# Scores of both head groups in one piece of TensorE, the first batch by halves, and product 1 of the next block between products 5 and 3

## The chip, the core and the metric

The program runs on one core of a Trainium2 chip. The metric is the device time of one execution in microseconds (us), the median of several executions. A core has TensorE (PE, matmuls; its weight loads are listed apart as PEld), VectorE (DVE), ScalarE (ACT), GpSimd (POOL), and SyncE (SP), which here issues all DMAs. They run side by side and wait for each other by semaphores; each works through its own instructions in a fixed order.

## What is computed

Attention over 32 memory slots, then two feed-forward layers, all in float32:

```python
a = softmax(phi, axis=2)                          # (8 batches, 8 heads, 576 tokens, 32 slots)
k_m = einsum('bhsm,bhsd->bhmd', a, k); v_m = einsum('bhsm,bhsd->bhmd', a, v)
scores = matmul(q, k_m.transpose(0, 1, 3, 2)) / sqrt(64)
x = matmul(softmax(scores), v_m)                  # tokens: 8 batches x 576, heads joined to 512
r = maximum(x @ w_in, 0);  x = (s * r * r + b) @ w_out      # 512 -> 2048 -> 512
h = x @ w1;  out = (h * sigmoid(1.702 * h)) @ w2            # 512 -> 2048 -> 512
```

(`softmax` stands for the reference's maximum, exponential and division by the sum plus 1e-9; `w1` and `w2` are the second layer's `moe2_w_in` and `moe2_w_out`.)

## The kernel before

The work has four stages, each of eight blocks; a block is one batch of 576 tokens, always handled as two halves of 288 columns (`HS`). Matmuls of full size keep two parts of each operand, a high and a low one, and take three passes: high·high, high·low, low·high. The conversions `hi` and `lo` that make these parts run on ACT or DVE.

- **Stage 1, attention and the first matrix.** For a batch and each of two groups `g` of four heads, `slots` makes the slot softmax and a tile `km` (64 rows of it per group hold the keys). `attend` multiplies `km` with the queries: eight small matmuls of 64 x 32 weights and 288 columns (rows of `km` given by `g`, columns by the head `p`, one half `u` of the tokens each), into one PSUM tile `a`; these are *the scores of one head group*. DVE turns them (`st`), takes the maximum, subtracts, ACT takes the exponential, DVE sums, divides and turns back (`aT`), and `hi` and `lo` make `ah` and `al`. `matrix` folds the values into the first weight matrix: eight matmuls of 64 x 32 and 512 columns into a PSUM tile `vw`, from which ACT makes `mh` and DVE `ml`; four times a batch. `step` then does 12 full-size matmuls (`mh`·`ah`, `mh`·`al`, `ml`·`ah`) into a PSUM tile `h`; ACT (or DVE) applies the maximum with zero and SP stores the result. There are 16 steps a batch. While batch b is in its steps, the slots and scores of batch b+1 are made.
- **Stages 2 and 4, `down`.** 2048 to 512 by seven products instead of eight (two levels of additions replace one product). Each product has four quarters `q` of 12 full-size matmuls. Products 1, 6, 5 and 3 add up in one PSUM tile X, 2 in Z, 7 and 4 in Y. After 1, 6 and 5, X is copied out by ACT before the next product may add to it: `leave` does it, in stage 2 with two ACT instructions (tiles `a`, `u2`, `u4`; `u` in the rows), in stage 4 with one.
- **Stage 3, `up`.** 512 to 2048 with the same seven products, in four quarters; the change does not touch it.

PSUM holds four tiles (`"ps": 4`, two banks each) for all of this. The order of everything is written out by a planner (class `Order`): each operation has a due time and a set of tiles that it reads and writes, and the planner assigns engine and place by its own costs. Where an operation can run on ACT or DVE, it takes the one with the smaller "start + cost x `WEIGHT`". So a due time or a weight moves many instructions. Before the first batch's steps, PE is kept busy with dummy matmuls (`warm`), which the planner puts into gaps until the operation `last` is placed.

Of the kernel before, what the change touches and what calls it, by code (L numbers as in the profile page):

```python
# [18 lines left out]
P = 128  # L19
# [8 lines left out]
class Order:  # L28
# [9 lines left out]
    LAG = {"pe": 0.7, "sync": 2.5, "dve": 0.25, "act": 0.25, "pool": 0.25}  # L38
    WEIGHT = {"dve": 1.0, "pool": 1.6, "act": 1.0}

# [112 lines left out]
class Net:  # L153
# [249 lines left out]
    def slots(self, b, g, due, lead=8):  # L403
# [42 lines left out]
        def norm():  # L446
            s = self.t(rs, [P, 1])
            nc.vector.tensor_scalar(s, T[z][:, 0, 128:129], EPS, None, op0=ALU.add)
            nc.vector.reciprocal(s, s)
            nc.vector.tensor_scalar(self.t(a, [P, P]), T[z][:, 0, 0:128], s, None, op0=ALU.mult)  # L450

        self.on_dve(d + 5, 60, norm, (z,), (a, rs), count=4)

# [8 lines left out]

    def attend(self, b, g, due):
        nc, T = self.nc, self.T
        S, J = self.S, self.S // 32
        qs = [("t", ("q", b, p)) for p in range(4)]
        if g == 0:
            for p, k in enumerate(qs):
                self.dma(due - 8 + 0.5 * p, lambda k=k: self.t(k, [P, S]), lambda p=p: self.a["q"][b, p], (), (k,))
        d = due  # L470
        ps, sm, sm2 = ((x, ("a", b, g, x)) for x in ("ps", "sm", "sm"))
        sm2 = ("sm", ("a2", b, g))
        st, aT = ("t", ("st", b, g)), ("t", ("aT", b, g))
        km, o = ("km", (b, g)), slice(64 * g, 64 * g + 64)

        def score():
            out = self.pst(ps)
            for u in range(2):
                for p in range(4):
                    w = slice(32 * p, 32 * p + 32)  # L480
                    nc.tensor.matmul(out[w, u, 0:self.HS], T[km][o, w], T[qs[p]][o, u * self.HS:(u + 1) * self.HS], start=True, stop=True)

        def turn():
            x = self.t(st, [P, J, 32]).rearrange("p J m -> p (J m)")
            for u in range(2):
                c = slice(u * self.HS, (u + 1) * self.HS)
                nc.vector.transpose(x[:, c], T[ps][:, u, 0:self.HS])

        def with_slots(e, m, op):
            e.tensor_tensor(T[st], T[st], T[m].unsqueeze(2).to_broadcast([P, J, 32]), op=op)  # L490
# [7 lines left out]
        self.pe(d, 2200, score, (*qs, km), (ps,))  # L498
        self.on_dve(d + 1, self.HS, turn, (ps,), (st,), count=2)
        self.on_dve(d + 2, S, lambda: nc.vector.tensor_reduce(self.t(sm, [P, J]), T[st], axis=AX.X, op=ALU.max), (st,), (sm,))  # L500
        self.on_dve(d + 2, S, lambda: with_slots(nc.vector, sm, ALU.subtract), (sm,), (st,), port=True)
        self.on_act(d + 3, S, lambda: nc.scalar.activation(T[st], T[st], AF.Exp, scale=0.125), (), (st,))
        self.on_dve(d + 4, S + 200, total, (st,), (sm2,))
        self.on_dve(d + 4, S, lambda: with_slots(nc.vector, sm2, ALU.mult), (sm2,), (st,), port=True)
        self.on_dve(d + 5, S, lambda: nc.vector.transpose(self.t(aT, [P, S]), T[st].rearrange("p J m -> p (J m)")), (st,), (aT,))
        ah, al = ("t", ("ah", b, g)), ("t", ("al", b, g))
        self.hi(d + 6, S, lambda: self.t(ah, [P, S], F32R), lambda: T[aT], (aT,), (ah,))
        self.lo(d + 6.5, S, lambda: self.t(al, [P, S], F32R), lambda: T[aT], lambda: T[ah], (aT, ah), (al,))

# [21 lines left out]
    def step(self, b, pi, u, due):  # L531
# [12 lines left out]

        self.pe(due, 12 * HS, mm, (*m, *ats[0], *ats[1]), (h,))
        self.order.add(due + 0.5, [
# [22 lines left out]
    def down(self, name, src, s, due, prior, first):  # L569
# [5 lines left out]
        G = [[("t", (x, name, s, q)) for x in "ABCDE"] for q in range(4)]  # L575
        pos = {1: 0, 2: 1, 6: 2, 7: 3, 5: 4, 3: 5, 4: 6}
        to = {1: X, 2: Z, 6: X, 7: Y, 5: X, 3: X, 4: Y}
# [172 lines left out]
    def warm(self, begin):  # L750
# [18 lines left out]
        else:  # L769
            self.pe(-5, 0, last, (x, ("t", ("al", 0, 0))))  # L770

    def plan(self):
# [8 lines left out]
        for b in range(B):  # L781
            s0 = b * B1
            if b == 0:
                for g in range(2):
                    self.slots(0, g, -42 + 4 * g, 10)
                    self.attend(0, g, -28 + 4 * g)
                self.warm(False)
            for j in range(4):
# [117 lines left out]
```

## Time and profile before

| | |
|---|---|
| median of 3 executions | 1437.73 us (1436.1 to 1439.28) |
| the profiled execution's own time | 1438.46 us |
| its span, first to last instruction | 1436.4 us |
| mean granted TensorE clock | 0.992 of full |
| stage 1 on PE | to 341.6 us |
| stage 2 on PE | 341.4 to 719.0 us |
| stage 3 on PE | 688.3 to 1076.2 us |
| stage 4 on PE | 1068.0 to 1432.4 us |

Times inside the trace count from the span's start. "Busy" is the time in which an engine had an instruction at work; PE's matmuls are pipelined, and their ends are modelled. A bracket at the end of a timeline row is idle time of that engine just before it, and the instruction whose end released it. PEclk is the granted share of TensorE's clock: 1.00 is 2.4 GHz, 0.50 is 1.2 GHz.

### The profile page before, as it was taken

Reading aid. Unit: us, or ns where it says so; the run is one execution under the profiler, and the core shown is the slowest. Engines: PE = TensorE matmul, PEld = TensorE weight load, DVE = VectorE, ACT = ScalarE, POOL = GpSimd, SP = SyncE. Lnnn points to the kernel's source line nnn. Section 1 sums busy time; section 2 is a strip of 40 time slices with the busy share of each in tenths; the row PEclk is TensorE's granted clock in tenths of the full one; section 3 lists DMA queues with packets and bytes.
Section 4 is the critical chain, followed back from the end, with each engine's and each line's share of the span. In section 5 each row is a group of like instructions: output and inputs, shape, how many; then the busy total and the mean of one; then the engine's idle time right before and its main releaser. Section 6 shows DMA issues by size and latency. Waiting matters only on the chain.

```text
span 1436.4 us, 28622 instructions
## 1 busy us (share of the span) xinstructions
PE 1400.5 (98%) x11190; PEld 1340.0 (93%) x11190; DVE 1098.2 (76%) x1728; ACT 762.4 (53%) x1224; POOL 94.7 (7%) x70
## 2 busy tenths in 40 slices
PE   6899999999999999999999999999999999999998
PEld 5778877789999999999999999999999999999998
DVE  7879998986898988898895565752458787777872
ACT  4455654566676666665565555554444434243441
POOL 1400110100101000100110010100000000000000
PEclk9899999999999999999999999999999999999999
DMA  9979999899954465475998756473598433554330
GB/s 354 322 258 340 353 322 344 289 309 366 313 181 131 140 238 149 156 256 171 346 347 318 278 180 239 169 266 133 188 357 310 127 116 108 156 157 131 114 104 34
DMA packets 136775, 329.19 MB, mean 229 GB/s; under 512 B 15552, under 2 KB 15552, under 8 KB 136640
## 3 DMA queue, kind: packets, MB, share of 16 engines
q1 hardware_dynamic: 136640, 327.37, 66.2%
q8 instruction: 88, 1.44, 0.4%
q14 instruction: 47, 0.39, 0.1%
HBM read 192.56 MB, written 134.74 MB: 228 GB/s over the span
## 4 chain that ended last, share of the span: by engine, by line
PE 50%; DMA 1%; DVE 0%; issue 0%; ACT 0%; SPq 0%; DVEq 0%
PE X L611 5%; PE X L613 5%; PE X L612 5%; PE X L718 5%; PE X L720 5%; PE X L719 5%; PE Y L611 3%; PE Y L613 3%; PE Y L612 3%; PE Y L718 2%; PE Y L720 2%; PE Y L719 2%; PE Z L611 1%; PE Z L613 1%; PE Z L612 1%; PE Z L718 1%
## 5 line engine op out<-in xcount | busy, mean ns | idle before, releaser
L263 PE MATMUL h<-ah,mh 128*128 128x288 f32 x512 | 160.5, 313 | 4.7 <-DVE ah L242 4.5
L265 PE MATMUL h<-ah,ml 128*128 128x288 f32 x512 | 154.3, 301 | 9.3 <-DVE ml L247 9.1
L611 PE MATMUL X<-oh,wo 128*128 128x288 f32 x512 | 152.7, 298 | 9.8 <-ACT u L637 9.7
L264 PE MATMUL h<-al,mh 128*128 128x288 f32 x512 | 154.2, 301 | 2.1 <-DVE al L247 2.1
L611 PE MATMUL X<-oh,w 128*128 128x288 f32 x512 | 151.7, 296 | 0.7 <-ACT u L631 0.7
L718 PE MATMUL X<-oh,w 128*128 128x288 f32 x512 | 151.7, 296 | 0.2 <-DMA w<-w 0.2
L612 PE MATMUL X<-ol,wo 128*128 128x288 f32 x512 | 151.6, 296 | 0.0
L719 PE MATMUL X<-ol,w 128*128 128x288 f32 x512 | 151.1, 295 | 0.3 <-DVE ol L247 0.3
L612 PE MATMUL X<-ol,w 128*128 128x288 f32 x512 | 151.0, 295 | 0.0
L613 PE MATMUL X<-oh,wo 128*128 128x288 f32 x512 | 151.0, 295 | 0.0
L720 PE MATMUL X<-oh,w 128*128 128x288 f32 x512 | 150.5, 294 | 0.0
L613 PE MATMUL X<-oh,w 128*128 128x288 f32 x512 | 150.5, 294 | 0.0
L247 DVE TENSOR_TENSOR h<-Y,u 128x576 f32<-128x576 f32 x64 | 48.4, 757 | 128.7 <-ACT u L726 89.5
L547 ACT ACTIVATE r<-h 128x576 f32<-128x576 f32 x122 | 79.5, 651 | 110.2 <-PE h L265 90.8
L263 PEld LDWEIGHTS h<-ah,mh 128*128 128x128 f32 x512 | 99.8, 195 | 26.7 <-ACT r L547 12.0
L247 DVE TENSOR_TENSOR ol<-C,oh 128x576 fp32r<-128x576 f32 x128 | 94.9, 753 | 21.5 <-ACT oh L241 11.4
L265 PEld LDWEIGHTS h<-ah,ml 128*128 128x128 f32 x512 | 99.2, 194 | 10.5 <-DVE ml L247 10.5
L241 ACT CAST oh<-A 128x576 fp32r<-128x576 f32 x106 | 68.1, 672 | 74.3 <-PE Y L613 29.8
L611 PEld LDWEIGHTS X<-oh,wo 128*128 128x128 f32 x512 | 96.2, 188 | 11.7 <-ACT u L637 11.7
L247 DVE TENSOR_TENSOR ol<-A,oh 128x576 fp32r<-128x576 f32 x128 | 94.7, 760 | 15.3 <-PE X L613 5.7
L264 PEld LDWEIGHTS h<-al,mh 128*128 128x128 f32 x512 | 99.2, 194 | 2.9 <-DVE al L247 2.9
L746 ACT ACTIVATE g<-h 128x576 f32<-128x576 f32 x96 | 65.8, 686 | 67.5 <-DVE h L247 64.4
(181 smaller groups left out, 4226.8 us busy)
## 6 DMA issues: line engine op xcount, KB each, us to landing
w<-w SPq DMA_DIRECT2D x112, 512.0 KB, 5.7
r<-r SPq DMA_DIRECT2D x128, 288.0 KB, 4.1
g<-g SPq DMA_DIRECT2D x128, 288.0 KB, 2.7
wo<-wo SPq DMA_DIRECT2D x42, 512.0 KB, 5.2
kv<-in_kv SPq DMA_DIRECT2D x64, 258.0 KB, 4.8
raw<-in_w SPq DMA_DIRECT2D x32, 512.0 KB, 6.1
q<-in_q SPq DMA_DIRECT2D x32, 288.0 KB, 4.9
A<-r SPq DMA_DIRECT2D x32, 288.0 KB, 3.2
```

The costliest lines, as they stand in the source:

```text
L241: self.order.add(due, [self.act(n, lambda: nc.scalar.copy(out(), src()), psum), self.dve(n, lambda: nc.vector.tensor_copy(out(), src()), f ...
L247: self.order.add(due, [self.dve(n, lambda: nc.vector.tensor_tensor(out(), a(), b(), op=op), port=port)], r, w, first)
L263: self.nc.tensor.matmul(ps, wh, xh, start=start and i == 0, stop=False)
L264: self.nc.tensor.matmul(ps, wh, xl, start=False, stop=False)
L265: self.nc.tensor.matmul(ps, wl, xh, start=False, stop=(i == n - 1))
L547: self.act(2 * HS, lambda: nc.scalar.activation(self.two(r), T[h][:, :, 0:HS], AF.Relu), psum=True),
L611: nc.tensor.matmul(out, T[w][:, 0, c], T[h][:, p], start=f, stop=False, skip_group_check=True)
L612: nc.tensor.matmul(out, T[w][:, 0, c], T[l][:, p], start=False, stop=False, skip_group_check=True)
L613: nc.tensor.matmul(out, T[w][:, 1, c], T[h][:, p], start=False, stop=last, skip_group_check=True)
L718: nc.tensor.matmul(out, T[w][:, 0, c], T[h][:, k], start=f, stop=False, skip_group_check=True)
L719: nc.tensor.matmul(out, T[w][:, 0, c], T[l][:, k], start=False, stop=False, skip_group_check=True)
L720: nc.tensor.matmul(out, T[w][:, 1, c], T[h][:, k], start=False, stop=k == 1, skip_group_check=True)
```

## The change

Four things are edited.

1. `attend` takes both head groups at once. One PSUM tile holds the scores of one half of the tokens for both groups, and a pair of matmuls that use the two row halves of the array stands side by side. For the batches after the first, both halves are one operation of 16 matmuls, due 18 us into the block; before, the two groups were due at 18 and 25 us. The softmax is in a new function `weigh`, for any set of halves.
2. For the first batch the two halves are separate: own scores, own softmax, own `ah` and `al` columns (half-size instructions). Steps read the halves they need. The first `matrix` is due 16 us earlier, and the dummy matmuls end when the first half's `al` and the first `ml` are there.
3. In `slots` the division may run on ACT, and DVE's `WEIGHT` is 2.0 instead of 1.0, so that the planner gives more to ACT.
4. In `down`, product 1 of a block is due three places earlier, between products 5 and 3 of the block before; in the last block product 2 is put between 5 and 3. Weights of stage 2 are due 12 us earlier.

```diff
-    WEIGHT = {"dve": 1.0, "pool": 1.6, "act": 1.0}
+    WEIGHT = {"dve": 2.0, "pool": 1.6, "act": 1.0}
...
-        self.on_dve(d + 5, 60, norm, (z,), (a, rs), count=4)
+        self.on_dve(d + 5, 30, norm, (z,), (rs,), count=2)
+        self.order.add(d + 5, [self.act(128, lambda: scale(True), psum=True), self.dve(190, lambda: scale(False))], (z, rs), (a,))
...
-    def attend(self, b, g, due):
+    def attend(self, b, due, groups, apart):
...
+        for n, us in enumerate(groups):
+            d = due + apart[1] * n
+            ps = {u: ("ps", ("a", b, u)) for u in us}
+
+            def score(us=us, ps=ps):
+                for u in us:
+                    out = self.pst(ps[u])
+                    for p in range(4):
+                        w = slice(32 * p, 32 * p + 32)
+                        for g in range(2):
+                            o = slice(64 * g, 64 * g + 64)
+                            nc.tensor.matmul(out[w, g, 0:HS], T[kms[g]][o, w], T[qs[p]][o, u * HS:(u + 1) * HS], start=True, stop=True)
+
+            self.pe(d, 2200 * len(us) // 2, score, (*qs, *kms), tuple(ps.values()))
+            for g in range(2):
+                self.weigh(b, g, us, ps, d, apart[0] * g)
...
-        pos = {1: 0, 2: 1, 6: 2, 7: 3, 5: 4, 3: 5, 4: 6}
+        pos = {1: -3, 2: 0, 6: 1, 7: 2, 5: 3, 3: 5, 4: 6}
+        if s == self.B - 1:
+            pos = {1: -3, 6: 0, 7: 1, 5: 2, 2: 3, 3: 4, 4: 5}
...
-            self.pe(-5, 0, last, (x, ("t", ("al", 0, 0))))
+            self.pe(-5, 0, last, (x, ("t", ("al", 0, 1), 0), ("w", ("ml", 0, 0))))
...
-                    self.attend(0, g, -28 + 4 * g)
-                self.warm(False)
+                self.attend(0, -28, ((0,), (1,)), (2, 6))
...
-                self.matrix(b, j, d - 8)
+                self.matrix(b, j, d - (24 if b == j == 0 else 8))
...
-                elif b + 1 < B:
-                    self.attend(b + 1, j - 2, s0 + 18 + 7 * (j - 2))
+                elif b + 1 < B and j == 2:
+                    self.attend(b + 1, s0 + 18, ((0, 1),), (4, 0))
...
-                self.weights("wo", i, q, t2 - 12 + 6.2 * (1, 2, 6, 7, 5, 3, 4).index(i) + q * 1.5)
+                self.weights("wo", i, q, t2 - 24 + 6.4 * (1, 2, 6, 7, 5, 3, 4).index(i) + q * 1.5)
```

Counted over the built programs, DVE has 1638 instructions of the kernel where it had 1728, and ACT 1332 where it had 1222; PE has the same matmuls but for 12 more dummy ones, and SP issues the same DMAs.

**On PE, the scores of batch 2, the third batch.** Before, one head group stands alone: `a` is its PSUM tile, `km_1125` its keys, `q_...` the queries of the four head pairs. The other group's eight follow three steps later.

```order
L456 MATMUL s_1249<-ident,an_1241 128x128
L481 MATMUL a_1253<-q_847,km_1125 32x288
L481 MATMUL a_1253<-q_889,km_1125 32x288
L481 MATMUL a_1253<-q_892,km_1125 32x288
L481 MATMUL a_1253<-q_912,km_1125 32x288
...
L263 MATMUL h_1269<-ah_914,mh_1152 128x288
```

Now the keys of both groups (`km_1188`, `km_1314`) alternate, and the second tile `a_1341` follows at once:

```order
L489 MATMUL a_1332<-q_827,km_1188 32x288
L489 MATMUL a_1332<-q_827,km_1314 32x288
L489 MATMUL a_1332<-q_833,km_1188 32x288
L489 MATMUL a_1332<-q_833,km_1314 32x288
...
L489 MATMUL a_1341<-q_916,km_1188 32x288
L489 MATMUL a_1341<-q_916,km_1314 32x288
L263 MATMUL h_1362<-ah_966,mh_1186 128x288
```

Two pieces of PE became one. From its end to the first step of the next batch there are now seven steps and two `matrix` pieces; before, there were five steps and two `matrix` pieces after the second group.

**On DVE, the first batch.** Before, the first `ml` stands behind the whole softmax of both groups and behind parts of a weight conversion (`wi`):

```order
L505 STREAM_TRANSPOSE aT_383<-st_313 128x576
L242 CAST ah_387<-aT_383 128x576
L247 TENSOR_TENSOR al_391<-aT_383,ah_387 128x576
L299 TENSOR_SCALAR wi_289<-wi_289 128x512
L302 SCALAR_TENSOR_TENSOR wi_289<-raw_249,wi_289 128x512
L296 TENSOR_SCALAR wi_289<-wi_289 128x512
L247 TENSOR_TENSOR ml_404<-vw_299,mh_323 128x1024
```

Now it stands inside the second half's softmax (`st_351`, `st_353` are the second half of the two groups, `ah_333` the first group's `ah`, whose second half is made here):

```order
L511 TENSOR_TENSOR st_351<-st_351,a_74_373 128x288
L511 TENSOR_TENSOR st_353<-st_353,a_370 128x288
L247 TENSOR_TENSOR ml_385<-vw_305,mh_327 128x1024
L537 STREAM_TRANSPOSE aT_392<-st_351 128x288
L242 CAST ah_333<-aT_392 128x288
```

From DVE's first transposition of scores to this `ml` there were 26 instructions: 14 of 576 columns, 4 of 288, 4 of the weight conversion and 4 small ones. Now there are 29: 23 of 288 columns and 6 small ones. Up to the second `ml` (of the next `matrix`), the softmax had 14 instructions of 576 columns, 4 of 288 and 4 small ones; it has 30 of 288 and 8 small ones, and 4 small ones of `slots` have come before that `ml`. The conversion pieces up to there are the same 19 and the two reductions of `slots` too.

**On PE, from product 5 to product 3 of the first block in stage 2.** Before, product 3 (`oh_4871`) follows product 5 (`oh_4865`) on the same PSUM tile `X_4614`:

```order
L612 MATMUL X_4614<-ol_4970,wo_3886 128x288
L613 MATMUL X_4614<-oh_4865,wo_3886 128x288
L611 MATMUL X_4614<-oh_4871,wo_4781 128x288
L612 MATMUL X_4614<-ol_4975,wo_4781 128x288
L613 MATMUL X_4614<-oh_4871,wo_4781 128x288
```

Now two quarters of the next block's product 1 (tile `X_5061`, 24 matmuls) stand between the last quarter of product 5 and the first of product 3 (tile `X_4492`):

```order
L646 MATMUL X_4492<-ol_4973,wo_3967 128x288
L647 MATMUL X_4492<-oh_4910,wo_3967 128x288
L645 MATMUL X_5061<-oh_4979,wo_3901 128x288
...
L647 MATMUL X_5061<-oh_4993,wo_3923 128x288
L645 MATMUL X_4492<-oh_4996,wo_4734 128x288
L646 MATMUL X_4492<-ol_5081,wo_4734 128x288
```

Over the eight blocks of stage 2, the number of other quarters between such neighbours was, from 6 to 5: 2, 2, 0, 2, 2, 2, 0, 3, and from 5 to 3: 0, 1, 0, 2, 2, 0, 2, 1. It is now 2, 2, 3, 2, 2, 3, 3, 2 and 2, 2, 2, 2, 2, 1, 1, 2. In stage 4, from 5 to 3, it was 1 in seven blocks and 0 in the last; it is now 0 in the first and the last and 1 in the others.

## Rows read from the trace of the kernel before

**Rows 1.** The page: busy time and share of each engine.
```profile
PE 1400.5 (98%) x11190; PEld 1340.0 (93%) x11190; DVE 1098.2 (76%) x1728; ACT 762.4 (53%) x1224; POOL 94.7 (7%) x70
```
**Rows 2.** Waits of PE over the span: us in total, times, longest.
```profile
PE X L611 <- ACT u L637: 9.7, 6, 2.6
PE h L265 <- DVE ml L247: 9.1, 3, 6.5
PE X L611 <- ACT u L631: 0.7, 1, 0.7
```
**Rows 3.** Timeline of PE, small matmuls: start us, us, what, [idle before].
```profile
20.72 2.00 PE L481 MATMUL a<-q,km 64*32 64x288 f32 x32
22.54 2.01 PE L524 MATMUL vw<-wi,km 64*32 64x512 f32 x16
...
61.66 1.09 PE L524 MATMUL vw<-wi,km 64*32 64x512 f32 x16
62.68 1.09 PE L439 MATMUL s<-kv,ph 128*32 128x129 f32 x32
...
63.95 1.15 PE L481 MATMUL a<-q,km 64*32 64x288 f32 x16
65.03 0.40 PE L263 MATMUL h<-ah,mh 128*128 128x288 f32 x1
```
**Rows 4.** Windows: busy us (instructions) by engine, then PEclk, DMA share, GB/s.
```profile
22.70:53.00 30.30, 19.40 (x162) 14.72 (x153) 27.91 (x48) 20.20 (x33) 8.83 (x7) 0.83 0.90 318
53.00:84.00 31.00, 30.32 (x286) 24.29 (x286) 28.19 (x54) 16.03 (x24) 8.16 (x7) 0.94 0.99 371
196.50:200.20 3.70, 3.67 (x17) 3.67 (x18) 3.56 (x7) 0.65 (x1) 0.28 (x1) 0.57 0.94 290
480.00:500.00 20.00, 20.00 (x152) 20.00 (x152) 19.30 (x30) 13.93 (x24) 0.00 (x0) 1.00 0.24 83
606.00:609.90 3.90, 3.85 (x18) 3.85 (x19) 3.41 (x5) 1.72 (x3) 0.00 (x0) 0.58 0.44 134
```
**Rows 5.** Timeline of PE and DVE, the first batch.
```profile
38.26 0.61 PE L265 MATMUL h<-ah,ml 128*128 128x288 f32 x1 [6.53 <-DVE ml L247]
53.07 0.40 PE L265 MATMUL h<-ah,ml 128*128 128x288 f32 x1 [2.02 <-DVE ml L247]
...
22.70 0.85 DVE L487 STREAM_TRANSPOSE st<-a 128x288 f32<-128x288 f32 x2 [0.71 <-PE a L481]
36.99 1.22 DVE L247 TENSOR_TENSOR ml<-vw,mh 128x1024 fp32r<-128x1024 f32 x1
51.80 1.22 DVE L247 TENSOR_TENSOR ml<-vw,mh 128x1024 fp32r<-128x1024 f32 x1
83.35 0.76 DVE L247 TENSOR_TENSOR al<-aT,ah 128x576 fp32r<-128x576 f32 x1
```
**Rows 6.** Groups by line: busy us, mean ns, idle before.
```profile
L490 DVE TENSOR_TENSOR st<-st,a 128x576 f32<-128x576 f32 x32 | 24.2, 758 | 0.8
L413 DVE TENSOR_REDUCE an<-ph 128x128 f32<-128x640 f32 x16 | 21.0, 1318 | 2.9 <-DMA ph<-in_phi 2.9
L637 ACT ACTIVATE u<-X,bw,sc 128x288 f32<-128x288 f32 x32 | 17.7, 585 | 5.1 <-PE X L613 5.1
```
**Rows 7.** Timeline of PE, where a batch of stage 1 begins.
```profile
195.73 0.40 PE L263 MATMUL h<-ah,mh 128*128 128x288 f32 x1 [1.47 <-DVE ah L242]
235.98 0.40 PE L263 MATMUL h<-ah,mh 128*128 128x288 f32 x1 [1.44 <-DVE ah L242]
275.44 0.40 PE L265 MATMUL h<-ah,ml 128*128 128x288 f32 x1 [0.59 <-DVE ml L247]
```
**Rows 8.** Timeline of PE and ACT in stage 2, at copies of X.
```profile
373.56 0.29 PE L613 MATMUL X<-oh,wo 128*128 128x288 f32 x1
375.01 0.40 PE L611 MATMUL X<-oh,wo 128*128 128x288 f32 x1 [1.17 <-ACT u L637]
375.25 0.29 PE L612 MATMUL X<-ol,wo 128*128 128x288 f32 x1
...
705.91 0.40 PE L611 MATMUL X<-oh,wo 128*128 128x288 f32 x1 [0.83 <-ACT u L637]
...
603.21 0.68 ACT L585 ACTIVATE B<-B 128x576 f32<-128x576 f32 x1 [1.90 <-DMA B<-r]
604.95 1.05 ACT L637 ACTIVATE u<-X,bw,sc 128x288 f32<-128x288 f32 x2
```

More of the change, by code (lines that the diff above doesn't have):

```diff
@@ L449, in norm, with scale @@
             nc.vector.reciprocal(s, s)
-            nc.vector.tensor_scalar(self.t(a, [P, P]), T[z][:, 0, 0:128], s, None, op0=ALU.mult)
-        self.on_dve(d + 5, 60, norm, (z,), (a, rs), count=4)
+        def scale(act):
+            x = self.t(a, [P, P])
+            if act:
+                nc.scalar.activation(x, T[z][:, 0, 0:128], AF.Copy, scale=T[rs])
+            else:
+                nc.vector.tensor_scalar(x, T[z][:, 0, 0:128], T[rs], None, op0=ALU.mult)
+        self.on_dve(d + 5, 30, norm, (z,), (rs,), count=2)
+        self.order.add(d + 5, [self.act(128, lambda: scale(True), psum=True), self.dve(190, lambda: scale(False))], (z, rs), (a,))
         def turn():
@@ L460, in slots @@
         self.hi(d + 6, 128, lambda: T[km], lambda: T[tr][:, 0, 0:P], (tr,), (km,), psum=True)
-    def attend(self, b, g, due):
-        nc, T = self.nc, self.T
-        S, J = self.S, self.S // 32
+    def attend(self, b, due, groups, apart):
+        nc, T, S, HS = self.nc, self.T, self.S, self.HS
         qs = [("t", ("q", b, p)) for p in range(4)]
[L467 to L481, printed above, removed]
+        kms = [("km", (b, g)) for g in range(2)]
+        for p, k in enumerate(qs):
+            self.dma(due - 8 + 0.5 * p, lambda k=k: self.t(k, [P, S]), lambda p=p: self.a["q"][b, p], (), (k,))
+        for n, us in enumerate(groups):
[12 more added lines that the diff above has]
+                self.weigh(b, g, us, ps, d, apart[0] * g)
@@ L483, in turn, with weigh @@
+    def weigh(self, b, g, us, ps, d, later):
+        nc, T, HS = self.nc, self.T, self.HS
+        n = HS * len(us)
+        J = n // 32
+        sm, sm2 = ("sm", ("a", b, g, us)), ("sm", ("a2", b, g, us))
+        st, aT = ("t", ("st", b, g, us)), ("t", ("aT", b, g, us))
+        ah, al = ("t", ("ah", b, g)), ("t", ("al", b, g))
+        cols = slice(us[0] * HS, us[0] * HS + n)
         def turn():
             x = self.t(st, [P, J, 32]).rearrange("p J m -> p (J m)")
-            for u in range(2):
-                c = slice(u * self.HS, (u + 1) * self.HS)
-                nc.vector.transpose(x[:, c], T[ps][:, u, 0:self.HS])
@@ L489, in with_slots @@
-        def with_slots(e, m, op):
-            e.tensor_tensor(T[st], T[st], T[m].unsqueeze(2).to_broadcast([P, J, 32]), op=op)
+            for i, u in enumerate(us):
+                nc.vector.transpose(x[:, i * HS:(i + 1) * HS], T[ps[u]][:, g, 0:HS])
+        def with_slots(m, op):
+            nc.vector.tensor_tensor(T[st], T[st], T[m].unsqueeze(2).to_broadcast([P, J, 32]), op=op)
         def total():
@@ L496, in total, with part, keys, made @@
             nc.vector.reciprocal(m, m)
[L498 to L508, printed above, removed]
+        def part(k):
+            if us[0] == 0:
+                self.t(k, [P, self.S], F32R)
+            return T[k][:, cols]
+        def keys(k):
+            return tuple((*k, u) for u in us)
+        def made(k):
+            return ((*k, 0),) if us[0] else ()
+        self.on_dve(d + 1 + 0.5 * g, HS, turn, tuple(ps.values()), (st,), count=len(us))
+        d += later
+        self.on_dve(d + 2, n, lambda: nc.vector.tensor_reduce(self.t(sm, [P, J]), T[st], axis=AX.X, op=ALU.max), (st,), (sm,))
+        self.on_dve(d + 2, n, lambda: with_slots(sm, ALU.subtract), (sm,), (st,), port=True)
+        self.on_act(d + 3, n, lambda: nc.scalar.activation(T[st], T[st], AF.Exp, scale=0.125), (), (st,))
+        self.on_dve(d + 4, n + 200, total, (st,), (sm2,))
+        self.on_dve(d + 4, n, lambda: with_slots(sm2, ALU.mult), (sm2,), (st,), port=True)
+        self.on_dve(d + 5, n, lambda: nc.vector.transpose(self.t(aT, [P, n]), T[st].rearrange("p J m -> p (J m)")), (st,), (aT,))
+        self.hi(d + 6, n, lambda: part(ah), lambda: T[aT], (aT, *made(ah)), keys(ah))
+        self.lo(d + 6.5, n, lambda: part(al), lambda: T[aT], lambda: T[ah][:, cols], (aT, *keys(ah), *made(al)), keys(al))
     def matrix(self, b, j, due):
@@ L543, in mm @@
                 self.mm3(out[:, i, 0:HS], [([T[x][:, k, o] for x in m], [T[x][:, c] for x in ats[k]]) for k in range(2)])
-        self.pe(due, 12 * HS, mm, (*m, *ats[0], *ats[1]), (h,))
+        self.pe(due, 12 * HS, mm, (*m, *((*x, u) for k in ats for x in k)), (h,))
         self.order.add(due + 0.5, [
@@ L799, in plan @@
                 d = s0 + j * B1 / 4
-                self.matrix(b, j, d - 8)
+                self.matrix(b, j, d - (24 if b == j == 0 else 8))
+                if b == j == 0:
+                    self.warm(False)
                 for i in range(2):
```

## Prediction

> **What bounds the kernel now.** The page comes first: PE is busy 98% of the span, DVE 76%, ACT 53% [rows 1]. So PE sets the end, and only three things can shorten the run: less work on PE, less idle time on PE, or less time at half clock. The table of PE's waits comes next. Of its larger entries one is the copy of X by ACT in stage 2, 9.7 us in 6 waits; one is `ml` in stage 1, 9.1 us in 3, of which 6.5 is a single wait; stage 4 has one of 0.7 us [rows 2]. Then the windows: in an undisturbed stretch PE does 152 full-size matmuls in 20 us, 0.1316 us each, so a step or a quarter of 12 takes 1.58 us in the window from 480 us [rows 4]. In windows after a wait of 1.5 to 2.6 us the granted clock is near 0.5, that is 1.2 GHz for part of them: 17 matmuls in 3.70 us should have taken 2.24, so 1.46 us are lost, and 18 in 3.90 us lose 1.53 [rows 4].
>
> **The scores on PE.** Eight matmuls of one head group (16 instructions in the trace) take from 63.95 to 65.03, 1.08 us; two groups apart take 2.16 [rows 3]. They use one row half of the array. How a piece that uses both row halves runs, `vw` shows: 16 instructions of 512 columns from 61.66 to 62.68, 1.02 us, though its columns are 1.78 times those of the score piece [rows 3]. The new pair has 32 instructions of 288 columns, 1.125 times the columns of `vw`: 1.15 us. It saves 1.0 us a batch. The first batch has both groups adjacent already, 20.72 to 22.54, 1.82 us [rows 3]; were the new pair no better than that, it would save 0.34. I take 1.0, because in the order now the row halves alternate as they do inside `vw`. Only batches 2 to 7 count, six of them, since the first two are made while DVE bounds the start (next part): -6.0 us, with ends at -2.0 and -6.5 (a pair as quick as one group alone).
>
> **The first batch.** PE stops 6.53 us for the first `ml` and again 2.02 for the second [rows 5]. The first goes to 36.99 + 1.22 = 38.21, 15.5 us after DVE's first transposition at 22.70. In the new order 29 instructions stand before it. A half-size transposition takes 0.42 (0.85 for two) [rows 5], a full-size operation 0.76 [rows 6]; with 0.42 for each of the 23 half-size ones, an estimated 0.2 for each of 6 small ones and 1.2 for `ml` it is 12.1 us. DVE can start some 0.7 us earlier, in its idle time at 22.70, as the first half's scores are ready sooner: the first `ml` lands near 34.1, and the first step gains 4 us. But the step after it needs the second half's `al`, seven half-size pieces, two small ones and a conversion later (some 4.9 us): 39. And the second `ml`, at 53.02 before [rows 5], has in front of it 30 half-size pieces at 0.42 and 12 small ones at 0.2 where there were 14 full-size at some 0.72 (their pace back to back), 4 half-size and 4 small: 15.0 against 12.6, so 2.4 us more. DVE was busy 27.91 of 30.30 us up to there, and 28.19 of the next 31.00 [rows 4]; a late start of the conversions is not made up. The second `ml` lands at 53.02 - 0.7 + 2.4 = 54.7 if DVE's idle time stays, at 52.3 if it goes. The first batch's end, where `al` lands at 83.35 + 0.76 = 84.11 [rows 5], is then as before: 0 us, with ends at -4 (the first step's gain kept) and +2.
>
> **The begin of the other batches.** PE waits 1.47, 1.44 and 0.59 us there [rows 7], each costs 0.27 more than its bracket (next part), and after the first two the clock is low, 1.46 us by the window and the same taken for the other: 7.2 us in all. Now both groups' softmax runs in one stretch. On DVE: four transpositions at 0.42, for each group six pieces of 576 columns at 0.76 (subtraction, two reductions, product, turning back, `al`; `ah` has gone to ACT but for one) and an estimated 0.4 of small ones; over both groups 1.7 + 9.1 + 0.8 = 11.6, and two `ml` at 1.2 within it: 14.0 us. PE meanwhile has seven steps at 1.58 and two `matrix` pieces at 1.02: 13.1, plus 0.4 until the second group's `ah` is needed and 0.6 since DVE may begin with the first half's tile: 14.1. The two are level, so it depends on what else DVE has queued. There it has less than before: 90 instructions fewer in the program, most in this stage. I leave 3.2 of the 7.2 us in place: -4 us. The ends: -7.2 (no wait left) and +15.2 (each of seven batches loses 3.2, as the one at 195.73 does with its low clock: 22.4 - 7.2).
>
> **PSUM.** The new pair fills two tiles of four at once. DVE needs 4 x 0.42 for them, perhaps behind a reduction of 1.32 [rows 6], 3.0 us; the step after the pair takes one free tile, and the next one, 1.6 us later, may have to wait up to 1.4 us if the fourth tile is still `vw`. The trace of before shows no such wait of PE. Seven pairs: 0 to +10 us. I take +1, near the lower end, since the row of before nearest to it (`vw`, read by ACT and DVE for longer than scores are) delays no step.
>
> **Stage 2 and 4.** At 375.01 PE waited 1.17 us by the bracket, but start to start from 373.56 and on to 375.25 it is 1.69 us for two matmuls, 0.26 normal, so a wait costs its bracket plus 0.26 [rows 8]. Six waits: 9.7 + 1.6 = 11.3, and the low clock at 606 us 1.5: 12.8 us. A copy is two instructions of 0.585 us, 1.05 together [rows 6, 8], and behind other ACT work it can be later: before the 2.6 us wait ACT stood 1.90 us for a load of `B`, with `u` behind it [rows 8]. In the order now every such pair has at least one other quarter between (1.58 us) and all but two have two or more (3.16 us), which covers the longest wait of before. For the two with one quarter I take 0.6 each, between nothing and the 0.83 + 0.26 of 705.91, which had one quarter between too [rows 8]: 1.2 stays. What is late next there is Y: product 4 needs Y read by DVE after `u4`, but a quarter of product 3 lies before it as before. In stage 4, the first block has lost its quarter between 5 and 3: +1.0 us (the 0.7 of rows 2 and 0.26); the last keeps its own. Sum -10.6, with ends at -13.5 and -4. The loads of product 1 go out up to three places, 19 us by due time, earlier in SP's queue; in SP's order now, 19 stores of stage 1 stand between the first block's loads and the step beside which its product 1 runs, and within stage 2 the DMAs have room (share 0.24 in the window from 480 us [rows 4]), so I cost them at nothing; were a load late, PE would stand for it, at most some 3 us.
>
> **More on ACT.** 110 instructions more on an engine that is idle 47% of the span [rows 1]: nothing while PE bounds. Its price is in the copies of X: a cast in front delays one; two quarters cover that.
>
> **Sum.** 1438.46 (the profiled execution) - 6.0 + 0 - 4.0 + 1.0 - 10.6 = 1418.9. The median of the runs is 0.73 lower, so the forecast is 1418 us.
>
> **Rivals.**
> (a) *The queue of steps at each new batch.* Place: the first step of batches 1 to 7, at the wait for the second group's `ah`. For it: 14.0 against 14.1 us, no reserve; against it: counted in the order of before by the same durations, DVE had 22 us of work, weight preparation included, between the first group's scores and the places at 195.73 and 235.98, against 19 on PE, and PE lost only some 1.5 there. With 3.2 us at each of the seven: 1418 + 19 = 1437, no change. It decides for slower from 3.7 us each on (7 x 3.7 = 25.9): 1440.5 and above.
> (b) *PSUM.* PE stands after each pair of scores because two tiles are full at once and DVE alone empties them: seven times 1.4 instead of 1 in all, 1427. The Trainium skill states this as a rule against such a change (TensorEngine Tiling (Array Packing), section PSUM Bottleneck): tiling speeds up TensorE and not the emptying of PSUM, which may become the bottleneck. By that rule the sum would be 1427; the trace of before does not bear it out after `vw`, but never had two such tiles in a row.
> (c) *The wait in stage 2 only moves.* The copies come late because ACT, which works in order, stands for a load or has more casts in front; more cover then hides less. If the waits stay 0.83 to 1.2 us at half of the places, 6 us of the 12.8 stay: 1423. For it: the 1.90 us at 603.21; against it: nothing in the order puts a load of the same block there, and two quarters are 3.16 us.
> (d) *All of it works,* the first step's gain too, and no wait at a batch: 1418 - 4 - 3.2 - 1 = 1410.
> (e) *The pair of scores is not faster* than when adjacent (0.34 us): 1422.
>
> **How the numbers follow.** Forecast as it stands, with (e) and (c) as its neighbours: 0.66 together (0.42, 0.12, 0.12); (d) 0.13; (b) 0.10; (a) 0.11, of which 0.04 near no change and 0.07 slower. The forecast's own range is 1411 to 1424. For 8 in 10 I go from 1408 to 1431: it leaves out most of (a) and the best ends of (d). Faster by over 0.2%, 2.9 us, which is about what a measurement of this kernel tells from no change: 0.89; within it 0.04; slower 0.07.
>
> **What would show it.** PE's small matmuls: one piece of scores per batch, near 1.1 us, and no row of it twice. Waits of PE: the entry for `u` in stage 2 under 2.5 us (it was 9.7), and a new one of about 0.7 us in stage 4's first block. First batch: the wait for `ml` shorter, but the step after the second `ml` still starting at 52 to 55 us, and batch 1 near 84. Begin of batches: brackets on `ah` or `al` under 1 us. Windows at 1.2 GHz: none in stage 2. The forecast is wrong if batch beginnings show brackets over 2 us again and again, or if steps just after the pair wait for DVE's transpositions.

## The result, and the profile after

The changed kernel takes 1415.93 us (median of 4 runs, 1413.07 to 1417.85), the kernel before 1437.65 on the same chip: a ratio of 0.9847, interval 0.9825 to 0.9869. The forecast was 1418, the range 1408 to 1431. The profiled execution took 1414.63 us, 23.8 less than the 1438.46 of before.

The page's first rows, which answer to [rows 1]:

```profile
span 1412.6 us, 28715 instructions
PE 1386.7 (98%) x11214; PEld 1336.8 (95%) x11214; DVE 1057.5 (75%) x1638; ACT 822.7 (58%) x1334; POOL 95.7 (7%) x70
```

PE still sets the end, with 13.8 us less at work; DVE lost 40.7 us of work, ACT gained 60.3. The table of PE's waits, against [rows 2] (us in total, times, longest):

```profile
PE h L265 <- DVE ml L247: 7.4, 4, 3.6
...
PE h L264 <- DVE al L247: 1.9, 3, 0.8
...
PE X L645 <- ACT u L665: 1.5, 2, 0.7
...
PE X L645 <- ACT u L671: 0.6, 1, 0.6
```

The 9.7 us for the copy of X in stage 2 have become 0.6 (line 671 is that copy now), the longest wait for `ml` 3.6 instead of 6.5.

To see where the 23.8 us went, the span is cut at three matmuls that both kernels have: the first of batch 1, the first of batch 7, the last of all. In the trace of before the first two are

```profile
82.93 0.38 PE L263 MATMUL h<-ah,mh 128*128 128x288 f32 x1
...
313.44 0.40 PE L263 MATMUL h<-ah,mh 128*128 128x288 f32 x1
```

and in the trace of after

```profile
86.14 0.40 PE L263 MATMUL h<-ah,mh 128*128 128x288 f32 x1
...
300.76 0.40 PE L263 MATMUL h<-ah,mh 128*128 128x288 f32 x1
```

The last matmul starts at 1432.08 before and at 1408.01 after. So the start is 3.2 us longer, the six batches between (230.5, now 214.6) are 15.9 shorter, and the rest (1118.6, now 1107.3) is 11.4 shorter. All experiments below are cut in the same way.

**The six batches.** The view of windows for before, first all instructions, then those of the scores' tile `a` alone (busy us and instructions of PE, PEld, DVE, ACT, then POOL where there is any, PEclk, DMA share, GB/s):

```profile
82.93:313.44 230.51, 225.63 (x2260) 183.38 (x2260) 205.98 (x354) 126.21 (x198) 21.69 (x16) 0.99 0.90 313
...
82.93:313.44 230.51, 14.07 (x192) 4.98 (x192) 51.46 (x96) 0.00 (x0) 0.99 0.90 313
```

and the same for after:

```profile
86.14:300.76 214.62, 212.65 (x2268) 178.79 (x2260) 187.12 (x320) 143.96 (x234) 21.54 (x16) 1.00 0.95 339
...
86.14:300.76 214.62, 7.15 (x192) 3.43 (x192) 50.84 (x96) 0.00 (x0) 1.00 0.95 339
```

The same 192 score matmuls keep PE busy for 7.15 us instead of 14.07. DVE has 18.9 us less work, ACT 17.8 more. PE idles for 2.0 us (214.62 less 212.65, of which 1.9 at two begins) instead of 4.9. The stretch at half clock near 197 us [rows 4] is gone, and so is a second one, in the windows of before

```profile
238.10:241.30 3.20, 3.20 (x15) 3.18 (x15) 2.99 (x5) 0.89 (x2) 0.00 (x0) 0.50 1.01 381
```

PEclk is now 1.00 for the whole of the six batches. A piece of scores in the timeline of PE, against [rows 3]:

```profile
22.02 1.64 PE L489 MATMUL a<-q,km 64*32 64x288 f32 x32
...
106.47 1.20 PE L489 MATMUL a<-q,km 64*32 64x288 f32 x32
107.60 0.40 PE L263 MATMUL h<-ah,mh 128*128 128x288 f32 x1
```

Both groups take 1.13 us from start to start, as much as one group of before (1.08). The step after shows no bracket. What is left at the begins of batches, against [rows 7]:

```profile
122.60 0.40 PE L263 MATMUL h<-ah,mh 128*128 128x288 f32 x1 [0.71 <-ACT ah L241]
123.39 0.40 PE L264 MATMUL h<-al,mh 128*128 128x288 f32 x1 [0.40 <-DVE al L247]
...
263.98 0.40 PE L265 MATMUL h<-ah,ml 128*128 128x288 f32 x1 [0.77 <-DVE ml L247]
```

**The first batch.** Timeline of PE and DVE, against [rows 5]:

```profile
35.16 0.40 PE L265 MATMUL h<-ah,ml 128*128 128x288 f32 x1 [3.56 <-DVE ml L247]
37.57 0.61 PE L264 MATMUL h<-al,mh 128*128 128x288 f32 x1 [0.67 <-DVE al L247]
39.82 0.61 PE L264 MATMUL h<-al,mh 128*128 128x288 f32 x1 [0.79 <-DVE al L247]
54.40 0.61 PE L265 MATMUL h<-ah,ml 128*128 128x288 f32 x1 [2.18 <-DVE ml L247]
...
33.88 1.22 DVE L247 TENSOR_TENSOR ml<-vw,mh 128x1024 fp32r<-128x1024 f32 x1
39.31 0.45 DVE L247 TENSOR_TENSOR al<-aT,ah 128x288 fp32r<-128x288 f32 x1
53.12 1.22 DVE L247 TENSOR_TENSOR ml<-vw,mh 128x1024 fp32r<-128x1024 f32 x1
```

The first `ml` comes 3.1 us earlier than before, but the step then stands for the second half's `al`, and the second `ml` is 1.3 us later. The clock in these places, in the windows of after:

```profile
38.40:43.40 5.00, 4.21 (x17) 3.85 (x17) 4.90 (x10) 3.37 (x6) 2.16 (x2) 0.50 1.00 370
...
53.80:57.20 3.40, 2.81 (x11) 2.81 (x12) 2.63 (x5) 0.00 (x0) 1.91 (x2) 0.50 1.04 402
57.20:60.60 3.40, 3.40 (x16) 3.40 (x16) 2.99 (x5) 1.80 (x3) 0.56 (x1) 0.50 1.07 382
...
480.00:500.00 20.00, 20.00 (x152) 20.00 (x151) 18.61 (x30) 15.44 (x28) 0.00 (x0) 1.00 0.86 278
```

PE runs at 1.2 GHz for 6.8 us after the second `ml`; in the trace of before the window from 57.20 to 60.60 has PEclk 1.00. That this differs between executions of the same kernel is shown with the changed kernel run again. In full pace nothing changed: 152 matmuls in 20 us.

**Stages 2 and 4.** PE's timeline has three waits for a copy of X, where there were seven:

```profile
591.86 0.40 PE L645 MATMUL X<-oh,wo 128*128 128x288 f32 x1 [0.58 <-ACT u L671]
...
1086.32 0.40 PE L645 MATMUL X<-oh,w 128*128 128x288 f32 x1 [0.73 <-ACT u L665]
...
1395.24 0.40 PE L645 MATMUL X<-oh,w 128*128 128x288 f32 x1 [0.73 <-ACT u L665]
```

They stand where only one quarter is between (the sixth block of stage 2; the seventh has one too and no wait) and where none is (stage 4, first and last block).

### The profile page after: what moved, and what is told of

Read it like the earlier page. It is cut to its first block, busy times and chain, and to the rows that moved or that the text cites. A ratio compares the mean times of both kernels' runs of the same rounds, so it can differ in the third digit from the quotient of the medians.

```text
span 1412.6 us, 28715 instructions
## 1 busy us (share of the span) xinstructions
PE 1386.7 (98%) x11214; PEld 1336.8 (95%) x11214; DVE 1057.5 (75%) x1638; ACT 822.7 (58%) x1334; POOL 95.7 (7%) x70
## 4 chain that ended last, share of the span: by engine, by line
PE 92%; DVE 4%; DMA 3%; ACT 1%; issue 0%; SPq 0%; ACTq 0%; DVEq 0%
PE X L645 9%; PE X L647 9%; PE X L646 9%; PE X L752 5%; PE Y L645 5%; PE Y L647 5%; PE X L754 5%; PE X L753 5%; PE Y L646 5%; PE h L263 4%; PE h L265 4%; PE h L264 4%; PE Y L752 2%; PE Z L645 2%; PE Z L647 2%; PE Y L754 2%
## 5 line engine op out<-in xcount | busy, mean ns | idle before, releaser
L578 ACT ACTIVATE r<-h 128x576 f32<-128x576 f32 x128 | 83.2, 652 | 62.8 <-PE h L265 52.4
L241 ACT CAST oh<-C 128x576 fp32r<-128x576 f32 x116 | 77.1, 674 | 64.2 <-PE X L646 29.1
```

What stands on the lines that cost most here:

```text
L241: self.order.add(due, [self.act(n, lambda: nc.scalar.copy(out(), src()), psum), self.dve(n, lambda: nc.vector.tensor_copy(out(), src()), f ...
L578: self.act(2 * HS, lambda: nc.scalar.activation(self.two(r), T[h][:, :, 0:HS], AF.Relu), psum=True),
```

## The experiments

Medians stand beside the kernel before on the same chip (1440.12, 1440.10 and 1439.11 us in three sets). The three stretches are from one profiled execution each, read as above; "six batches" is from the first matmul of batch 1 to that of batch 7, "rest" from there to the last matmul. "WEIGHT" is DVE's.

| kernel | median us | ratio and interval | batch 1 begins | six batches | rest |
|---|---|---|---|---|---|
| before | 1437.7 to 1440.1 | 1 | 82.93 | 230.5 | 1118.6 |
| changed | 1415.93 | 0.9847 (0.9825 to 0.9869) | 86.14 | 214.6 | 1107.3 |
| changed, again | 1418.02 | 0.9842 (0.9815 to 0.9870) | 83.71 | 214.6 | 1106.9 |
| products alone | 1423.50 | 0.9888 (0.9870 to 0.9906) | 81.83 | 230.5 | 1103.9 |
| WEIGHT alone | 1425.47 | 0.9900 (0.9883 to 0.9918) | 83.16 | 221.5 | 1114.4 |
| scores alone | 1434.81 | 0.9962 (0.9949 to 0.9975) | 86.93 | 222.5 | 1120.7 |
| products undone | 1419.00 | 0.9853 (0.9835 to 0.9872) | 84.31 | 214.5 | 1114.0 |
| WEIGHT undone | 1422.03 | 0.9872 (0.9851 to 0.9892) | 89.51 | 224.0 | 1104.6 |
| first batch whole | 1410.27 | 0.9792 (0.9775 to 0.9808) | 81.01 | 214.6 | 1108.1 |
| groups in turn | 1418.33 | 0.9852 (0.9830 to 0.9873) | 86.76 | 215.6 | 1106.6 |
| scores later | 1424.56 | 0.9891 (0.9875 to 0.9907) | 84.69 | 220.7 | 1108.8 |
| whole, WEIGHT in stage 1 | 1406.30 | 0.9771 (0.9750 to 0.9792) | 81.99 | 214.6 | 1103.3 |
| the same, scores earlier | 1419.46 | 0.9860 (0.9845 to 0.9875) | 86.09 | 222.3 | 1105.7 |

**The changed kernel again.** 

> The changed kernel itself, to stand beside the others on one chip: 0.985 of the kernel before, as measured.

Its median is 1418.02; the profiled execution took 1411.73, with batch 1 at 83.71 instead of 86.14 and the other stretches as they were. So the six batches are read to 0.1 us, while the start moves by 2 to 3 us between executions. Most of that is half clock. From the end of the second `ml` to batch 1, the windows of the changed kernel, of the same kernel again, and of the run with the products undone (the same first batch) are

```profile
54.34:86.14 31.80, 30.05 (x279) 24.34 (x279) 26.60 (x45) 16.74 (x26) 8.15 (x7) 0.90 0.90 329
54.69:83.71 29.02, 27.27 (x279) 21.57 (x279) 27.30 (x46) 16.17 (x26) 8.16 (x7) 1.00 0.94 342
53.76:84.31 30.55, 28.80 (x280) 23.09 (x280) 27.16 (x45) 16.72 (x26) 8.13 (x7) 0.94 0.89 325
```

The first and the second stand behind the same wait; for the same kernel again it is (timeline of PE)

```profile
54.75 0.40 PE L265 MATMUL h<-ah,ml 128*128 128x288 f32 x1 [2.18 <-DVE ml L247]
```

Before that, DVE needs 31.1 to 31.2 us from its first transposition of scores to the end of the second `ml` in all five profiled executions with the halves and WEIGHT 2.0, so that part does not vary; the first transposition itself starts between 22.6 and 23.8. The other three executions of this run took 1417.6 to 1419.5, some 6 to 8 more than the profiled one, and where they lost it no trace shows. Stretches and medians are therefore compared apart in what follows.

**Products alone, and products undone.** In the kernel before:

```diff
-        pos = {1: 0, 2: 1, 6: 2, 7: 3, 5: 4, 3: 5, 4: 6}
+        pos = {1: -3, 2: 0, 6: 1, 7: 2, 5: 3, 3: 5, 4: 6}
```

with the last block's row and the due times of the weights as in the change; undone is the same edit turned round in the changed kernel.

> The kernel before with the order of the products alone (product 1 of the next block between 5 and 3, weights of stage 2 due earlier); the rest as before. Theory (the X copies were waited for because nothing stood between the neighbours on X): in this order every neighbouring pair on X in stages 2 and 4 has one or more quarters between; PE's 9.7 us on the copy u in stage 2 fall to under 1.5, the low clock near 606 us goes, stage 1 stays: 11 to 13 us less than before, about 1425.5. Rival (the copies come in time because ACT and DVE share the casts otherwise, the WEIGHT): half of the waits stay, 1431 to 1437.

> The changed kernel with the old order of the products. Three neighbouring pairs on X in stage 2 have nothing between (first block 5 to 3, sixth block 5 to 3, seventh block 6 to 5). Theory: each costs 1.4 to 2.9 us as before, perhaps with a stretch at 1.2 GHz (1.5 us): 7 to 11 us slower than the changed kernel, 1423 to 1427. Rival (WEIGHT does it): waits on u under 1 us each, 1417 to 1419.

Alone it gives 16.6 us, more than the 11 to 13 expected, and the table of PE's waits has no entry for a copy of X any more. The rest is 14.8 shorter, the first two stretches are about those of before. Undone, PE waits for the copies again:

```profile
PE X L643 <- ACT u L669: 7.8, 6, 2.3
```

The rest is 6.8 us longer for it. The median missed the 1423 to 1427 expected: it rose by only 1.0 to 3.1 us (1419.0 beside 1418.0 and 1415.9). In the profiled execution 1.8 us of the difference are a shorter start; for the others no trace tells. So the order of products takes the waits away, and in the traces it is worth 6.8 us with WEIGHT 2.0 and 14.8 with 1.0; with WEIGHT 2.0 the medians show less.

**WEIGHT alone, WEIGHT undone, scores alone.** One line, `"dve": 2.0` or `"dve": 1.0`; the scores alone are the changed kernel with the first batch whole, old products and WEIGHT 1.0 (the earlier first `matrix` and the division on ACT or DVE in `slots` stay in).

> The kernel before with DVE's weight at 2.0 and nothing else of the change. Theory (DVE's load made the waits at the begin of batches): the waits of 1.47 and 1.44 us near 196 and 236 us go, with the stretches at 1.2 GHz behind them, 5 to 7 us; in stage 2 the waits on the copies stay, since their neighbours stay: 5 to 9 us less than before. Rival (only together with the joint scores does it matter): within 2 us of before.

> The changed kernel with DVE's weight back at 1.0, so that some 130 instructions go back to DVE. Theory (DVE's load in stage 1 decides whether a batch's ah and al are in time): waits on ah or al at the begin of batches come back in the batches with weight preparation, 1.5 us each and some at 1.2 GHz, 3 to 7 us in all; stage 4 gets its quarter between 5 and 3 back in the first and last block, 2 us less: 1417 to 1421. Rival (DVE's load does not matter, PE bounds): 1413 to 1415, the 2 us of stage 4 alone.

> The scores of both groups in one piece for every batch, the first included, and nothing else of the change: DVE's WEIGHT 1.0, products and weights due as before. Theory (the parts overlap; one piece instead of two is worth 1.1 us of TensorE in each of batches 2 to 7, whatever the other parts do): TensorE's batches 1 to 7 take 6 to 7 us less from begin to begin than before less what the waits at the begins grow; with WEIGHT 1.0 those were 2.06, 3.46 and 1.52 us against 1.47, 1.44 and 0.59 before, some 4 us more; the waits for u in stage 2 stay near 10 us. So 1431 to 1437 beside 1440 of the kernel before. Rival (the scores bring their gain by themselves, waits at the begins as before): 1430 or less. Rival (the new length of the softmax stretch takes it all back): 1440 or more.

In the six batches the two parts stand almost in full beside each other: WEIGHT alone -9.0, scores alone -8.0, both -15.9. With WEIGHT undone the waits at the begins are back, longer than in [rows 7] (timeline of PE):

```profile
198.28 0.40 PE L265 MATMUL h<-ah,ml 128*128 128x288 f32 x1 [2.06 <-DVE ml L247]
...
237.49 0.40 PE L265 MATMUL h<-ah,ml 128*128 128x288 f32 x1 [3.46 <-DVE ml L247]
...
276.60 0.40 PE L263 MATMUL h<-ah,mh 128*128 128x288 f32 x1 [1.52 <-DVE ah L242]
```

So the scores in one piece don't cure the begins; DVE's smaller load does: in the six batches PE waits 6.5 us with the scores alone and 1.0 with WEIGHT alone, against 4.7 before. For the whole program the scores alone gave 4.3 us by the medians, 1.9 by the profiled executions: they lost 4.0 at the start (PEclk is 0.87 there from the second `ml` on, 0.94 before) and 2.1 in the rest.

Two expectations were missed. WEIGHT alone gave 14.6 us by the medians where 5 to 9 were expected, since it helps in stage 2 too: PE's waits for the copy of X fell from 9.7 to 5.7 us, and the rest is 4.2 shorter. So the rival to the products was right in part, and the parts of the change don't add up. With the new products there is nothing left of these waits to save, and WEIGHT 2.0 has a price: the rest is 1104.6 at 1.0 and 1107.3 at 2.0. WEIGHT undone came out at 1422.03, just above the 1417 to 1421 expected, with 9.4 us more in the six batches instead of 3 to 7. The division on ACT and the earlier first `matrix` were not run by themselves, so their share is not shown.

**The first batch whole.**

```diff
-                self.attend(0, -28, ((0,), (1,)), (2, 6))
+                self.attend(0, -28, ((0, 1),), (4, 0))
```

The dummy matmuls here end with the second half's `al` and the first `ml`.

> The changed kernel with the first batch's softmax not by halves (both halves in one operation, as in the other batches). Theory (DVE bounds the first 85 us, and the halves add some 2.5 us of work to it): the first step comes later than 35 us, but the second ml ends 1 to 3 us earlier than 54.3 and batch 1 begins 1 to 3 us earlier than 86: 1413 to 1415. Rival (the halves pay by the earlier first step): 2 to 4 us slower than the changed kernel, 1418 to 1420.

It is 5.7 us faster than the changed kernel by the medians, more than expected. In the profiled executions it lies before batch 1 (81.01 instead of 86.14; 83.7 to 86.8 in all five with the halves and WEIGHT 2.0). The timeline of PE:

```profile
33.60 0.61 PE L265 MATMUL h<-ah,ml 128*128 128x288 f32 x1 [2.18 <-DVE ml L247]
...
50.70 0.61 PE L265 MATMUL h<-ah,ml 128*128 128x288 f32 x1 [2.23 <-DVE ml L247]
```

The first `ml` is not later without the halves (33.60 against 35.16, within what starts differ by), and the second is 3.7 us earlier. The halves are a loss, and the shorter wait at the first step is there without them. What they cost with WEIGHT 2.0 is DVE's time from its first transposition to the end of the second `ml`: 31.1 to 31.2 us with them, 28.9 without, here and in the run with WEIGHT in stage 1 alone. With WEIGHT 1.0 that stretch is 31.0 us for a whole batch (scores alone) and 31.15 by halves (WEIGHT undone). Of the 5.1 us between 81.01 and 86.14 that is 2.2; 1.5 are a later first transposition, and 1.4 come after the second `ml`, where the changed kernel's execution had 3.4 us more at half clock.

**Groups in turn.** The same 32 score matmuls with all of group 0 ahead of group 1, instead of the alternation:

```diff
-                for u in us:
+                for g in range(2):
+                    for u in us:
...
-                        for g in range(2):
```

> The changed kernel, with the 16 score matmuls of a batch in another order: all eight of the first head group (one row half of the array), then all eight of the second. Theory (a pair is fast since matmuls on the two row halves stand side by side): the piece takes 1.8 us, as the first batch's in the kernel before, and not 1.1; 0.7 us more in each of six or seven batches, 4 to 5 us slower than the changed kernel. Rival (TensorE overlaps the two groups in any order, or the gain came from one piece instead of two): the piece stays at 1.1 to 1.3 us and the time within 1 us.

The rival holds. The six batches are 1.0 us longer, 0.2 a piece, against 0.7 or more that was expected of my reason; a piece before a step is (timeline of PE)

```profile
107.08 1.35 PE L490 MATMUL a<-q,km 64*32 64x288 f32 x32
108.37 0.40 PE L263 MATMUL h<-ah,mh 128*128 128x288 f32 x1
```

1.29 us, where two pieces apart are 2.16 [rows 3]. The two pieces that `vw` follows take 0.99 us in both orders. The median is that of the changed kernel. The gain is that the groups stand together; that their rows alternate is worth 0.2 us of the 1.1 at most.

**Scores later.**

```diff
-                    self.attend(b + 1, s0 + 18, ((0, 1),), (4, 0))
+                    self.attend(b + 1, s0 + 24, ((0, 1),), (4, 0))
```

> The changed kernel with the scores of the next batch due 24 us into the block instead of 18: six steps of TensorE instead of seven stand between them and the next batch, 1.58 us less, for the same work of DVE. Theory (with DVE's smaller load there is a reserve at most begins, below 1.6 us at batches 2 and 6, where the changed kernel still waits 0.7 to 0.8): the waits at batches 2 and 6 grow to some 2 to 3 us, the others stay under 1.6, +4 to +9 us against the changed kernel's 1416 to 1418: 1420 to 1427. Rival (a) of the prediction (both chains are level, no reserve): each of seven begins loses 1.6 to 3.2 us, 1428 to 1440. Rival (the reserve is larger than a step): within 2 us of the changed kernel.

The sum is as the theory had it (6.5 to 8.6 us above the changed kernel), the place is not. In the six batches 6.1 us are lost for a step of 1.58 taken out, 1.0 a batch on average, but unevenly: begin to begin the batches are 2.0, 0.1, 1.5, 0.8 and 2.5 us longer and the last 0.8 shorter. Of the 6.1 only 2.1 are more idle time of PE (4.0 instead of 1.9); the others are slower matmuls. And 2.7 of the 4.0 us are for `nm`, a maximum in `slots` of the batch after, which DVE does behind the softmax (timeline of PE):

```profile
158.40 0.29 PE L423 MATMUL s<-ident,nm 128*128 128x128 f32 x1 [0.80 <-DVE nm L422]
```

The waits for `ah` and `al` are 1.3 us there, where the changed kernel's steps wait 1.9. So the run shows what a step less costs, and not how large the reserve at the begins is.

**Whole first batch, WEIGHT 2.0 in stage 1 alone.** The planner's choice, with `until` the due time of stage 1's end:

```diff
-                    score = t + cost * self.WEIGHT.get(eng, 1.0)
+                    score = t + cost * (1.0 if eng == "dve" and due >= self.until else self.WEIGHT.get(eng, 1.0))
```

> The changed kernel with the first batch's softmax not by halves, and with DVE's weight of 2.0 for stage 1 alone, 1.0 from stage 2 on. Theory (the weight helps in stage 1, where DVE is full, and costs in stages 2 to 4, where it puts casts before the copies of X on ACT and leaves two neighbours in stage 4 with nothing between): losses behind stage 1 fall from 5 to 1 or 2 us, 3 to 4 us less than with the weight everywhere, 0.977 of before. Rival (the weight behind stage 1 is neutral): 0.979, as measured with it.

1406.3 us, a ratio of 0.9771: faster than both kernels. PE has no wait at all in the trace from 335 us on, and the rest is 4.0 us shorter than in the changed kernel.

**The same with scores earlier** (`s0 + 15`).

> The version with the first batch whole and DVE's WEIGHT 2.0 in stage 1 alone (1406.3 us beside 1440.1), with the scores of the next batch due 15 us into the block instead of 18; on TensorE seven steps stand between them and the next batch as before, so only DVE's and ACT's order differ. Theory (the 0.7 us waits left at the begins of batches 2 and 6 are from what DVE and ACT have queued, and the low-clock stretches and waits of the first 85 us are the rest): 1.5 to 3 us less, 1403 to 1405. Rival (these waits are from the length of the softmax stretch itself): no change, 1406.

Both missed: 13 us slower by the medians; in the traces the six batches are 7.7 longer, the start 4.1 and the rest 2.4. PE still has seven steps between scores and next batch, but DVE takes most of the first group's softmax ahead of the running batch's last `ml`. In the timeline of DVE and PE in batch 4:

```profile
218.39 1.57 DVE L508 STREAM_TRANSPOSE st<-a 128x288 f32<-128x288 f32 x4
...
225.55 1.19 DVE L247 TENSOR_TENSOR ml<-vw,mh 128x1024 fp32r<-128x1024 f32 x1
...
219.74 0.37 PE L263 MATMUL h<-ah,mh 128*128 128x288 f32 x1 [0.72 <-DVE st L508]
...
226.79 0.61 PE L265 MATMUL h<-ah,ml 128*128 128x288 f32 x1 [2.15 <-DVE ml L247]
```

In the kernel that this one was made from, the same `ml` stands 2.9 us behind the transpositions instead of 7.2, and PE does not wait for it (timeline of DVE):

```profile
208.96 1.56 DVE L508 STREAM_TRANSPOSE st<-a 128x288 f32<-128x288 f32 x4
...
211.87 1.22 DVE L247 TENSOR_TENSOR ml<-vw,mh 128x1024 fp32r<-128x1024 f32 x1
```

## Why the prediction was right, point by point

- **Scores on PE, -6.0:** the pieces of the six batches lost 6.9 us, just beyond the better end (-6.5). The size holds, the reason given does not: not the alternation makes the pair as quick as one group. The step that failed is the reading of `vw`, whose row halves do not alternate. `matrix` runs one row half and then the other:

  ```python
  for k in range(2):
      o = slice(64 - 64 * k, P - 64 * k)
      for c in range(4):
          ...
  ```

  So the 1.02 us of `vw` already spoke for a piece of two groups in turn. Nor was the 1.82 us of rival (e) the price of standing side by side: at that place the changed kernel's alternating piece takes 1.57 (22.02 to 23.59) and later 1.13, and the `vw` right behind in before is 2.01 us long and later 1.09 [rows 3]. Why small matmuls are slower there, at a granted clock of 1.00, no run shows.
- **The first batch, 0:** this step failed. Its marks came near (first `ml` landing at 35.1 for 34.1, the second half's `al` at 39.8 for 39, second `ml` at 54.3 for 54.7), the last one by luck: DVE began 0.5 us later than before (23.22 against 22.70) and not 0.7 earlier, and of its idle time up to there, which the sum left in, 1.4 of 2.4 us went. What failed is "the first batch's end is then as before": batch 1 begins 3.2 us later, beyond the end of +2. Of these 1.3 are the later second `ml` (54.40 against 53.07), and 1.9 come after it, where 3.4 us more pass at half clock; 16 instructions in such 3.4 us, by the pace of [rows 4] 2.1 us of work, are 1.3 lost. The term has no half clock in it, and that part goes with the execution: over five executions the term is 0.8 to 3.8. At an equal granted clock from the second `ml` on it is 1.4 to 1.9 (PEclk 0.94: 84.31 and 84.69 against 82.93; 1.00: 83.71 against the 81.83 of products alone, whose stage 1 is that of before). That is a loss too, inside the range stated.
- **The begins of the other batches, -4:** right in cause, too small. I left 3.2 of 7.2 us in place as a hedge and did not count three brackets of 0.40 for `al`. The six batches lost 15.9, of which 6.9 are the scores' busy time; the other 9.0 are 2.9 of idle time, the two half-clock stretches (1.46 by the window of [rows 4] and 1.23 by the one at 238.10), and some 3 us of slower matmuls beside waits and beside pieces that are now fewer, which I did not split further. WEIGHT alone gives the same 9.0. The reserve was counted as 14.0 against 14.1 us, level; the run with scores later does not settle it, since most of what PE waits there is for `nm`.
- **PSUM, +1:** no wait of PE behind a pair, so 0. Of the Trainium skill's rule (TensorEngine Tiling (Array Packing), section PSUM Bottleneck: after a fourfold speedup of TensorE by tiling, emptying PSUM may become the bottleneck) the trace of after shows nothing; the speedup of a piece here is 1.9, from 2.16 to 1.13 us. A wait for PSUM comes up where DVE is late with the two tiles: with scores earlier, a step waited 0.72 us for `st` at 219.74.
- **Stages 2 and 4, -10.6:** measured -11.4 from batch 7 on. This nearness is luck: the products alone are worth -14.8, beyond the better end of -13.5, and the next point takes 3.4 back. Of the two one-quarter places, priced at 0.6 each, one waited 0.58 and the other not; the first block of stage 4 was priced at 0.7 before the 0.26 and waited 0.73. No wait for a load appeared.
- **More on ACT, nothing:** wrong by some 2 to 5 us, hidden in the term before it. With WEIGHT 1.0 in stages 2 to 4 the same products give 1103.3 to 1104.6 instead of 1106.9 to 1108.1; I had priced ACT's load, not that the planner, with other costs, sets other products beside each other: with WEIGHT 2.0 three places have too little between, with 1.0 none of them waits.

The total came near because errors of opposite sign met. Against the profiled execution the sum was 4.3 us too high: the start erred by +3.2, the six batches by -6.9 (-15.9 for -9.0 with PSUM), the rest by -0.8. The medians differ by 2. Rival (a) is refuted as a loss: the begins improved. One step less costs 6 us, but mostly not at the wait that (a) names. (e) is refuted by the pieces, (c) by the waits of stage 2.

## What to carry to other kernels

Cut two traces at the same few instructions and compare stretches before comparing waits: here that showed an edit that costs 5.7 us by the medians, 2.2 of them as a longer stretch on DVE in the traces, inside a change that gains 22. Here a second group of small matmuls cost 0.05 to 0.2 us right behind the first and 1.08 on its own, so try putting such pieces together. Splitting an engine's work into halves to start earlier did not pay where that engine was the bound. A planner's weight is a change in every stage that it reaches, so set it per stage and look at each.

## What was not expected of the hardware

- 32 small matmuls in one piece cost 1.13 us alternating, 1.29 group after group, and 16 of one group alone 1.08 [rows 3]: nearly the same price for half and for all.
- The length of a wait alone does not tell whether half clock follows. In [rows 4, 7] it followed one of 1.47 us (with one of 0.40 behind it); with WEIGHT undone a wait of 2.06 was followed by full clock and one of 3.46 by half, in the windows of that kernel:

```profile
198.30:202.00 3.70, 3.70 (x28) 3.70 (x29) 3.56 (x7) 1.15 (x2) 0.23 (x1) 1.00 1.00 329
237.40:242.20 4.80, 4.71 (x24) 4.70 (x25) 4.08 (x6) 0.65 (x1) 0.00 (x0) 0.64 0.98 354
```

- In the same kernel, behind the same wait of 2.18 us for the second `ml`, 6.8 us at half clock followed in one execution and none in another; up to batch 1 the first took 2.8 us longer. In the five executions with that first batch the stretch from the second `ml` to batch 1 is 29.0 us with PEclk 1.00, 30.6 with 0.94 (two) and 31.8 with 0.90 (two).
